# Attention over chunks, then routed tokens: the first pairs of heads enter the planned order

## The chip, the cores and the metric

The kernel runs on one core of a Trainium2 chip. The metric is the device time in microseconds of one execution. The profile is of one execution and spans the first to the last instruction. The engines are TensorE (PE, with its weight loads as PEld), VectorE (DVE), ScalarE (ACT), GpSimd (POOL) and SyncE (SP). Each works its own list of instructions in order, and waits only for results of the others and for transfers.

## The reference

The inputs q, k and v have 4 batches, 8 heads, 768 rows and 64 columns; mem_k and mem_v have 8 memory rows for each head. Attention is done in chunks of 32 rows with 16 rows of context to the left and 8 to the right; the result is the x of a layer that routes 128 tokens of each batch through two matrices of 512x1024 and 1024x512.

```python
for c in range(nc):
    ...
    k_full = np.concatenate([mem_k, k_ctx], axis=2)
    v_full = np.concatenate([mem_v, v_ctx], axis=2)
    scores = scale * np.matmul(q_c, k_full.transpose(0, 1, 3, 2))
    ...
    a = a / (np.sum(a, axis=-1, keepdims=True) + 1e-09)
    out[:, :, c_start:c_end] = np.matmul(a, v_full)
...
scores = np.einsum('bsd,d->bs', x, w_gate)
for b in range(B):
    top_idx = np.argpartition(-scores[b], capacity)[:capacity]
    xe = x[b, top_idx]
    h = np.maximum(xe @ w1, 0.0)
    ye = h @ w2
    g = 1.0 / (1.0 + np.exp(-scores[b, top_idx]))
    out[b, top_idx] = x[b, top_idx] + g[:, None] * ye
```

## The kernel before

**Units of work.** Two heads of one batch make a pair; there are 16 pairs, 0 to 15, four to a batch. Two pairs make a load unit, 0 to 7: one transfer each for q, k and v, issued on GpSimd's queue, which turns fp32 into fp16 on the way. Unit 0 comes in halves, one for each pair. Four buffers hold the units of each tensor, so unit 4 of k can be fetched only when both pairs of unit 0 have used theirs.

**Steps of a pair n.** Each is a function s_... and its name stands in a written order with its arguments. Kt, Qt and Vt are 16 transposes each on TensorE (line 278), of k, q and v; Kt and Vt share one PSUM tile, p_t. Kc, Qc and Vc copy the results to SBUF (lines 299 or 297, 289, 319); Kc is on VectorE unless the name ends in @ACT, Qc and Vc on ScalarE. Km and Vm write the memory columns (line 303). S.n.half are the score products (line 356), E.n.half their exponentials, three activations on ScalarE (line 363). T2 turns v back (line 328), V2 copies that. VV.n.half is the product with v (line 382), X.n.half the division by the sum on VectorE: a reciprocal and a multiplication (lines 387 and 394). Pairs take turns in four slots of SBUF buffers (n modulo 4).

**Steps of a batch b.** ST.b stores x (lines 449 and 451, on SyncE). D.b.i are the gate's dot products (line 456), R0 and R1 with R0c and R1c lay the scores out as rows, C.b.i compares every score with every other (line 513), CT counts (line 529), M, P, SL and SE make the selection (lines 541 to 559), A and AI the row numbers (line 570), F gathers the rows from the output (line 576), XT and XC transpose them, F1, H, F2 and Y are the two matrices (lines 603 to 624), and SC adds the result into the output (line 627). GE and G are the gate. For the last batch the names differ: X15, S14, S15 (scores), RL, C3, CT3, P3, and G0 with GB in place of a gather.

**What sets the order.** ORDER (lines 19 to 49) is a list of step names; the loop at line 685 calls them one after another, and so each engine gets its instructions in this order. An ending @DVE, @ACT or @POOL moves a copy to that engine. LU.u.t issues the load of unit u of tensor t, LW.i one of eight loads of the weights (lines 246 and 249), wg the two loads of the gate vector on SyncE (lines 638 and 639), gc builds gate columns from it. fill-i-step puts i products with zeros ahead of a step on TensorE (line 155): work of no use but to keep its clock up.

**The start.** Pairs 0 and 1 are not in the list: lines 644 to 675 call their first steps by hand, with 25 fills among them, twelve of them ahead of Kt.0. The memory rows come in by two loads on GpSimd's queue, cast on the way (lines 139 and 141), between those of pair 0, and mem_rows (line 198) transposes each and lays it down in memkT and memvT.

Of the kernel before, what the change touches and what calls it, by code (L numbers as in the profile page):

```python
# [16 lines left out]


ORDER = """
S.1.1 Vm.3 fill-1-VV.0.0 VV.0.0 Vm.4@DVE E.1.1 S.1.0 X.0.0 LU.4.k Kt.2 E.1.0 fill-1-Qt.2 Qt.2 Kc.2 VV.0.1 Qc.2  # L20
Km.2@POOL Kt.3 X.0.1 wg LU.4.q S.2.0 T2.1 Kc.3 E.2.0 S.2.1 V2.1 Vt.2 E.2.1 Km.3 LU.4.v VV.1.1 Vm.5@DVE Qt.3 X.1.1 Vc.2
VV.1.0 Qc.3 LW.0 gc Vt.3 S.3.0 X.1.0 Vc.3 T2.2 S.3.1 V2.2 E.3.0 LW.1 Kt.4 Vm.6@DVE VV.2.0 Kc.4 E.3.1 T2.3 X.2.0 Vt.4
LU.5.k V2.3 VV.2.1 Vc.4 Vm.7 Km.4@DVE Qt.4 X.2.1 Kt.6 Qc.4 VV.3.0 LU.5.q Kc.6@ACT S.4.0 X.3.0 T2.4 E.4.0 Km.6 Kt.5
V2.4 VV.3.1 LU.5.v D.0.2 Kc.5@ACT Qt.5 D.0.1 fill-1-S.4.1 S.4.1 Qc.5 Km.5 D.0.0 Kt.7 LU.6.q E.4.1 X.3.1 fill-1-S.5.1
S.5.1 Qt.6 Kc.7 ST.0 E.5.1 VV.4.0 D.0.4 LW.4 S.5.0 Km.7 D.0.3 Vt.5 Qc.6 D.0.5 LU.6.v Vc.5 fill-1-R0.0 R0.0 Vm.8@DVE
X.4.0 S.6.1 GE.0 E.5.0 T2.5 G.0 Vt.6 Vm.9 V2.5 VV.4.1 Vc.6 LW.2 R0c.0@DVE S.6.0 Qt.7 X.4.1 E.6.1 Kt.8 LU.7.k R1.0 Kc.8
Qc.7 VV.5.0 R1c.0 Km.8 Vt.7 X.5.0 E.6.0 T2.6 C.0.1 S.7.1 Vc.7 VV.5.1 V2.6 S.7.0 LW.3 C.0.0 E.7.1 Qt.8 X.5.1 Vt.10 Qc.8
C.0.3 fill-1-VV.6.1 VV.6.1 C.0.2 Vc.10 fill-1-S.8.0 S.8.0 C.0.5 E.7.0 T2.7 Vm.10@DVE C.0.4 LU.7.q Kt.9 X.6.1 V2.7@ACT
CT.0 Vm.11 LU.7.v Kc.9@ACT fill-2-S.8.1 S.8.1 M.0 fill-1-VV.7.1 VV.7.1 E.8.1 Km.9@DVE LU.6.k Vt.8 X.7.1 Qt.9 Vc.8 P.0
D.1.4 VV.7.0 Qc.9 D.1.3 Vt.9 LW.5 SL.0 Vc.9 X.7.0 fill-1-T2.8 T2.8 SE.0.0 VV.6.0 SE.0.2 V2.8@ACT Vm.12 SE.0.5 SE.0.1  # L30
SE.0.3 Kt.10 SE.0.4 X.6.0 E.8.0 A.0 fill-1-Qt.10 Qt.10 AI.0 D.1.0 ST.1 F.0 VV.8.1 Qc.10 D.1.2 S.9.0 Kc.10@ACT S.9.1
X.8.1 LW.6 Qt.11 D.1.1 E.9.0 VV.8.0 Km.10@DVE D.1.5 R0.1 Qc.11 X.8.0 S.10.1 Kt.11 E.9.1 R0c.1@DVE T2.9 Kc.11 R1.1
E.10.1 Vm.13 V2.9 fill-1-S.10.0 S.10.0 Vt.11 R1c.1@DVE E.10.0 Km.11@DVE VV.9.0 C.1.5 S.11.0 C.1.3 Vc.11 T2.10 C.1.2
fill-1-S.11.1 S.11.1 Vm.14 V2.10@ACT X.9.0 Vt.12 XT.0 C.1.1 Vc.12 VV.9.1 C.1.0 T2.11 XC.0 X.9.1 LW.7 Kt.13 GE.1 E.11.0
G.1 Vm.15 VV.10.0 V2.11 F1.0.0 E.11.1 X.10.0 Qt.12 Kc.13 H.0.0 VV.11.0 Qc.12 C.1.4 Km.13 Kt.12 X.11.0 fill-1-CT.1 CT.1
Kc.12 D.2.0 Km.12 T2.12 D.2.1 fill-2-VV.11.1 VV.11.1 V2.12@ACT D.2.2 M.1 Vt.13 X.11.1 P.1 S.12.1 Vc.13 fill-1-S.12.0
S.12.0 SL.1 SE.1.0 SE.1.5 VV.10.1 SE.1.3 E.12.0 SE.1.1 SE.1.4 T2.13 SE.1.2 X.10.1 A.1 E.12.1 Kt.14 AI.1 ST.2 D.2.3
VV.12.0 F.1 V2.13@ACT D.2.5 F1.0.1 X.12.0 Kc.14@ACT Qt.13 D.2.4 VV.12.1 Qc.13 H.0.1@DVE Km.14 Kt.15 X.12.1 GE.2 R0.2
Kc.15 fill-1-S.13.0 S.13.0 G.2 R0c.2 S.13.1 E.13.0 Vt.14 Km.15@DVE R1.2 Qt.14 R1c.2@DVE Vc.14 VV.13.0 C.2.4 Qc.14
F2.0.0 C.2.1 C.2.0 E.13.1 T2.14 C.2.3 F2.0.1 V2.14@ACT C.2.5 C.2.2 S.14.1 Y.0 S.14.0 X.13.0 fill-1-GV.14 GV.14 E.14.0  # L40
SC.0 CT.2 D3.0 D3.1 E.14.1 GVc.14 fill-1-VV.13.1 VV.13.1 D3.2 M.2 Vt.15 X.13.1 P.2 fill-1-Qt.15 Qt.15 Vc.15 SL.2 D3.3
fill-1-VV.14.0 VV.14.0 SE.2.3 Qc.15 SE.2.0 SE.2.2 SE.2.1 D3.5 XT.1 X16a T2.15 SE.2.4 XC.1@DVE S.15.0 X.14.0 F1.1.1
E.15.0 V2.15 S.15.1 S14.0 GV.15 H.1.1 D3.4 fill-1-VV.14.1 VV.14.1 GVc.15 E.15.1 SE.2.5 VV.15.0 X.14.1 A.2 S15.0
VV.15.1 AI.2 X15.0 F1.1.0 F.2 S14.1 X16b.0 ST.3.0 S15.1 RL.0 H.1.0@DVE GE.3 fill-1-RL.1 RL.1 RLc.0 G.3 fill-1-F2.1.0
F2.1.0 C3.0.0 RLc.1 C3.1.0 C3.2.0 C3.0.1 F2.1.1 C3.2.1 C3.1.1 C3.3.2 fill-2-CT3.0 CT3.0 Y.1 C3.5.2 C3.4.2 SC.1
fill-1-XT.2 XT.2 X15.1 CT3.1 XC.2 ST.3.1 G0 X16b.1 M.3 F1.2.0 fill-3-P3 P3 H.2.0 F1.2.1 SL.3 SE.3.5 SE.3.4 SE.3.0
SE.3.1 GB.0 SE.3.3 H.2.1 SE.3.2 GB.4 GB.2 F2.2.0 GB.5 F2.2.1 GB.1 Y.2@DVE GB.3 XC.3 SC.2 A.3 F1.3.0 AI.3 F1.3.1 H.3.0
F2.3.0 H.3.1 F2.3.1 Y.3@DVE SC.3
""".split()
# [679 lines left out]
```

The softmax here doesn't subtract the row's maximum and nothing guards it: scores larger than these inputs give would overflow.

## Time and profile before

| | |
|---|---|
| time, median of 3 runs | 133.36 us (132.72 to 134.24) |
| span of the profiled execution | 132.6 us |
| busy: TensorE, VectorE, ScalarE, GpSimd | 110.8, 87.6, 85.8, 44.4 us |
| DMA: GpSimd's queue, SyncE's queue | 13.04 MB and 61.0% of the 16 engines; 6.56 MB and 16.6% |
| read from and written to HBM | 24.25 MB, 7.34 MB |
| mean granted TensorE clock | 0.936 |

The bytes of a queue in the profile are counted as they land: a load that casts reads twice what it writes. A line of the list of groups or of the timeline names the engine, the source line, the operation, output<-input with shapes, and in brackets how long the engine stood idle before it and what ended that. Busy times are averages over stages of different kinds: a load stage (to about 72 us), an attention stage (to about 104 us) and the last batch's chain of small steps (to the end).

### The profile page before, as it was taken

The page shows a single profiled execution, that of the slowest core. Times are in us where ns is not written, and L with a number is a line of the kernel's source. Part 1 is how long each engine was busy: PE and PEld are TensorE (multiplying, and loading weights), DVE is VectorE, ACT ScalarE, POOL GpSimd, SP SyncE. Part 2 cuts the span into 40 slices and gives each one's busy share as a digit, 9 for nine tenths or more (in the row PEclk, how much of TensorE's full clock was granted, in tenths as well). Part 3 has the DMA queues.
Part 4 walks back from the last instruction along what each step waited for, and adds up shares of the span by engine and source line. Part 5 has one row for each costly group of instructions (what it writes and reads, how often), then busy time and mean ns, then how long its engine had stood idle before and what let it go on. Part 6 is the DMA issues. An engine that isn't in the chain of part 4 may idle for free. (4 is left out here: it accounts for less than half of the span.)

```text
span 132.6 us, 4756 instructions
## 1 busy us (share of the span) xinstructions
PE 110.8 (84%) x2038; PEld 81.0 (61%) x2038; DVE 87.6 (66%) x295; ACT 85.8 (65%) x163; POOL 44.4 (33%) x73
## 2 busy tenths in 40 slices
PE   6998998999999109999899999999999975998300
...
DVE  3443678879998902279899999899969893311200
ACT  4037879989999406699999838889877523115000
...
PEclk9999999999999965899999999999869999599995
DMA  2899999999999999999998200990320475902350
GB/s 57 137 181 188 205 205 206 210 203 208 209 270 289 261 206 208 207 206 207 300 270 147 45 7 0 271 236 17 41 43 2 127 153 144 173 1 23 61 74 6
DMA packets 16085, 19.90 MB, mean 150 GB/s; under 512 B 1152, under 2 KB 11840, under 8 KB 16064
## 3 DMA queue, kind: packets, MB, share of 16 engines
q0 software_dynamic: 12416, 13.04, 61.0%
q1 hardware_dynamic: 3648, 6.56, 16.6%
...
HBM read 24.25 MB, written 7.34 MB: 238 GB/s over the span
## 5 line engine op out<-in xcount | busy, mean ns | idle before, releaser
L363 ACT ACTIVATE es<-pss_S,maskb 128x256 f16<-128x256 f32 x96 | 37.9, 495 | 3.2 <-PE pss_S L356 2.8
L382 PE MATMUL pxx_VV<-vc,es 128*96 128x65 f16 (+3 forms) x360 | 23.1, 207 | 1.6 <-DVE x L394 0.6
L382 PEld LDWEIGHTS <-es 128*32 128x32 f16 (+1 forms) x384 | 20.2, 113 | 6.4 <-DVE x L394 1.5
L319 ACT COPY vw<-p_t 128x960 f16<-128x960 f16 x16 | 15.5, 969 | 7.7 <-PE p_t L278 7.6
L289 ACT COPY qT<-pvv_Qt 128x768 f16<-128x768 f16 x16 | 13.1, 821 | 7.1 <-PE pvv_Qt L278 7.0
L394 DVE TENSOR_TENSOR x<-pxx_VV,rd 128x384 f32<-128x384 f32 x30 | 16.7, 557 | 1.0
L627 POOL DMA_INDIRECT out_dram<-y,idx x4 | 6.6, 1638 | 25.1 <-issue 7.2
L456 DVE SCALAR_TENSOR_TENSOR junk<-x,wgb 128x512 f32<-128x512 f32 (+1 forms) x24 | 14.5, 635 | 0.1
L513 DVE TENSOR_SCALAR gr<-brow,scr 128x768 f16<-128x768 f32 (+1 forms) x27 | 13.9, 570 | 0.1
L278 PE MATMUL p_t<-ident,v 96*64 96x96 f16 x256 | 8.8, 213 | 5.9 <-DMA v<-in_v_dram 5.9
L387 DVE RECIPROCAL rd<-pxx_VV 128x6 f32<-128x6 f32 x30 | 5.7, 190 | 10.5 <-PE pxx_VV L382 10.0
L278 PEld LDWEIGHTS <-v 96*64 96x64 f16 x256 | 6.6, 113 | 7.5 <-DMA v<-in_v_dram 6.5
L356 PE MATMUL pss_S<-qT,kw 64*128 64x96 f16 x256 | 10.6, 207 | 0.0
L328 PE MATMUL pvv_T<-ident,vw 128*128 128x128 f16 x128 | 10.5, 228 | 0.0
L155 PE MATMUL p_f<-zeros 128*128 128x512 f16 x25 | 9.1, 501 | 1.3 <-DVE zeros L149 1.3
L299 DVE COPY kw<-p_t 128x1024 f16<-128x1024 f16 x11 | 7.5, 685 | 3.2 <-PE p_t L278 3.2
L356 PEld LDWEIGHTS <-kw 64*128 64x128 f16 x256 | 6.4, 95 | 5.2 <-issue 3.6
L278 PE MATMUL pvv_Qt<-ident,q 96*64 96x96 f16 x256 | 8.8, 213 | 0.6 <-DMA q<-in_q_dram 0.6
L155 PEld LDWEIGHTS <-zeros 128*128 128x128 f16 x57 | 5.5, 110 | 6.0 <-issue 3.0
L603 PEld LDWEIGHTS <-w_sb 128*128 128x128 f16 x128 | 8.3, 106 | 1.4 <-issue 0.6
L328 PEld LDWEIGHTS <-vw 128*128 128x128 f16 x128 | 8.0, 102 | 1.6 <-ACT vw L319 0.2
L278 PE MATMUL p_t<-ident,k 96*64 96x96 f16 x256 | 8.7, 212 | 0.1
...
## 6 DMA issues: line engine op xcount, KB each, us to landing
...
```

Of the source, the lines that this page charges most:

```text
L155: nc.tensor.matmul(out=ap, lhsT=zeros[:, 0:128], rhs=zeros, start=True, stop=True)
L278: nc.tensor.transpose(out=dst[64 * h:64 * h + 64, j, :], in_=src[n][:, h, 64 * j:64 * j + 64], identity=ident16[0:96, 0:96])
L289: nc.scalar.copy(out=qT, in_=half_view(bank("Qt", n))[:, :, 0:96].rearrange("p j t -> p t j"))
L319: nc.scalar.copy(out=vws[n % SLOTS].rearrange("p g (j t) -> p g j t", t=16)[:, :, :, 0:15], in_=_sap(p_t, 0, [[12, NG], [100, 8], [1, 15]]))
L328: nc.tensor.transpose(out=p_v[:, g, :], in_=vws[n % SLOTS][:, g, :], identity=ident16)
L356: nc.tensor.matmul(out=p_s[:, h, 96 * gi:96 * gi + 96], lhsT=kw[o:o + 64, g, :], rhs=qf[o:o + 64, 96 * g:96 * g + 96], start=True, stop=True)
L363: nc.scalar.activation(out=es[:, :, :, 32 * c:32 * c + 32], in_=pv[:, :, :, 32 * c:32 * c + 32], func=AF.Exp, bias=maskb[:, c:c + 1], scal ...
L382: nc.tensor.matmul(out=p_x[r0:r1, i, h, :], lhsT=es[:, h, gi, q0:q1], rhs=vc[:, GROUPS[half][gi], h, 0:w], start=True, stop=True)
L394: nc.vector.tensor_tensor(out=xs[b].rearrange("p g (n h d) -> p n g h d", n=NP, d=D)[:, pr, 3 * half:3 * half + 3], in0=px_view(n, half)[: ...
L456: nc.vector.scalar_tensor_tensor(out=junk[:, 0:c1], in0=xs[b][:, bl, 0:c1], scalar=1.0, in1=wgb[:, 0:c1], op0=ALU.mult, op1=ALU.mult, accu ...
L513: nc.vector.tensor_scalar(out=once(b, "gr", [128, NB, S], F16)[:, bl, c0:c1], in0=m.brow[:, c0:c1], scalar1=m.scr[:, bl:bl + 1], scalar2=N ...
L603: nc.tensor.matmul(out=bank("F1", b, half)[:, 128 * fi:128 * fi + 128], lhsT=w1_sb[:, dch, f0:f0 + 128], rhs=get(b).xeT[:, dch, :], start= ...
```

## The change

The first steps of pairs 0 and 1 move from the hand-written start into ORDER, and the whole list is laid out anew, with other fills and some copies on other engines. What stays ahead of the list is six fills, the memory rows' transposes with three fills between, three Vm and two fills. The memory rows are loaded on SyncE as fp32 and cast to fp16 by two copies on ScalarE, which takes two loads off GpSimd's queue; the second mem_rows uses another PSUM tile than the first (pvv in place of pmm), so that it need not wait for it. In the list the loads now come unit by unit: 4, weights 0 and 1, 5, weights 2 and 3, 6, weights 4 and 5, 7, weights 6 and 7, where before unit 6 was split around unit 7. The aim is a start that is planned like the rest and loads that arrive in the order of their use. The same steps run as before.

```diff
 ORDER = """
-S.1.1 Vm.3 fill-1-VV.0.0 VV.0.0 Vm.4@DVE E.1.1 S.1.0 X.0.0 LU.4.k Kt.2 E.1.0 fill-1-Qt.2 Qt.2 Kc.2 VV.0.1 Qc.2
-Km.2@POOL Kt.3 X.0.1 wg LU.4.q S.2.0 T2.1 Kc.3 E.2.0 S.2.1 V2.1 Vt.2 E.2.1 Km.3 LU.4.v VV.1.1 Vm.5@DVE Qt.3 X.1.1 Vc.2
-VV.1.0 Qc.3 LW.0 gc Vt.3 S.3.0 X.1.0 Vc.3 T2.2 S.3.1 V2.2 E.3.0 LW.1 Kt.4 Vm.6@DVE VV.2.0 Kc.4 E.3.1 T2.3 X.2.0 Vt.4
-LU.5.k V2.3 VV.2.1 Vc.4 Vm.7 Km.4@DVE Qt.4 X.2.1 Kt.6 Qc.4 VV.3.0 LU.5.q Kc.6@ACT S.4.0 X.3.0 T2.4 E.4.0 Km.6 Kt.5
-V2.4 VV.3.1 LU.5.v D.0.2 Kc.5@ACT Qt.5 D.0.1 fill-1-S.4.1 S.4.1 Qc.5 Km.5 D.0.0 Kt.7 LU.6.q E.4.1 X.3.1 fill-1-S.5.1
-S.5.1 Qt.6 Kc.7 ST.0 E.5.1 VV.4.0 D.0.4 LW.4 S.5.0 Km.7 D.0.3 Vt.5 Qc.6 D.0.5 LU.6.v Vc.5 fill-1-R0.0 R0.0 Vm.8@DVE
-X.4.0 S.6.1 GE.0 E.5.0 T2.5 G.0 Vt.6 Vm.9 V2.5 VV.4.1 Vc.6 LW.2 R0c.0@DVE S.6.0 Qt.7 X.4.1 E.6.1 Kt.8 LU.7.k R1.0 Kc.8
-Qc.7 VV.5.0 R1c.0 Km.8 Vt.7 X.5.0 E.6.0 T2.6 C.0.1 S.7.1 Vc.7 VV.5.1 V2.6 S.7.0 LW.3 C.0.0 E.7.1 Qt.8 X.5.1 Vt.10 Qc.8
-C.0.3 fill-1-VV.6.1 VV.6.1 C.0.2 Vc.10 fill-1-S.8.0 S.8.0 C.0.5 E.7.0 T2.7 Vm.10@DVE C.0.4 LU.7.q Kt.9 X.6.1 V2.7@ACT
...
-E.15.0 V2.15 S.15.1 S14.0 GV.15 H.1.1 D3.4 fill-1-VV.14.1 VV.14.1 GVc.15 E.15.1 SE.2.5 VV.15.0 X.14.1 A.2 S15.0
-VV.15.1 AI.2 X15.0 F1.1.0 F.2 S14.1 X16b.0 ST.3.0 S15.1 RL.0 H.1.0@DVE GE.3 fill-1-RL.1 RL.1 RLc.0 G.3 fill-1-F2.1.0
-F2.1.0 C3.0.0 RLc.1 C3.1.0 C3.2.0 C3.0.1 F2.1.1 C3.2.1 C3.1.1 C3.3.2 fill-2-CT3.0 CT3.0 Y.1 C3.5.2 C3.4.2 SC.1
-fill-1-XT.2 XT.2 X15.1 CT3.1 XC.2 ST.3.1 G0 X16b.1 M.3 F1.2.0 fill-3-P3 P3 H.2.0 F1.2.1 SL.3 SE.3.5 SE.3.4 SE.3.0
-SE.3.1 GB.0 SE.3.3 H.2.1 SE.3.2 GB.4 GB.2 F2.2.0 GB.5 F2.2.1 GB.1 Y.2@DVE GB.3 XC.3 SC.2 A.3 F1.3.0 AI.3 F1.3.1 H.3.0
-F2.3.0 H.3.1 F2.3.1 Y.3@DVE SC.3
+Kt.0 Kc.0@ACT fill-2-Qt.0 Qt.0 Qc.0 Km.0 Vt.0 Vc.0 fill-2-S.0.0 S.0.0 fill-1-S.0.1 S.0.1 E.0.0 Kt.1 Qt.1 Kc.1 E.0.1
+Km.1 Vt.1 Qc.1 Vc.1 fill-4-S.1.1 S.1.1 S.1.0 E.1.1 T2.0 Kt.2 V2.0 E.1.0 Kc.2 fill-1-VV.0.0 VV.0.0 Vm.3@POOL Qt.2 X.0.0
+Km.2@POOL Kt.3 Qc.2 LU.4.k VV.0.1 Kc.3 Vm.4 Qt.3 Km.3 wg X.0.1 Vt.2 LU.4.q Qc.3 S.2.0 S.2.1 Vc.2 T2.1 LU.4.v E.2.1
+V2.1 Kt.4 Vm.5 Kc.4 fill-1-T2.2 T2.2 E.2.0 LW.0 Vt.3 V2.2 Vm.6 VV.1.0 Vc.3 gc Km.4 Qt.4 S.3.0 X.1.0 Qc.4 LW.1 Vt.5
+Vc.5 VV.2.1 S.4.1 X.2.1 E.3.0 T2.3 LU.5.k Vt.4 V2.3 E.4.1 VV.2.0 Vm.7@DVE S.4.0 X.2.0 Vc.4 fill-1-Qt.5 Qt.5 LU.5.q
+fill-1-VV.1.1 VV.1.1 E.4.0 Kt.5 X.1.1 Qc.5 S.3.1 LU.5.v Kc.5 VV.3.0 E.3.1 Km.5 Qt.6 X.3.0 Vt.7 Qc.6 LW.2 fill-1-S.5.0
+S.5.0 D.0.2 Vc.7 fill-1-VV.3.1 VV.3.1 D.0.0 D.0.1 E.5.0 T2.5 X.3.1 LW.3 Kt.8 V2.5@ACT fill-1-S.5.1 S.5.1 Vm.9 Kc.8
+ST.0 D.0.3 E.5.1 Kt.7 Km.8 D.0.5 Qt.7 LU.6.k VV.5.0 Kc.7@ACT D.0.4 R0.0 X.5.0 LU.6.q GE.0 Qc.7 Vt.6 G.0 VV.5.1 Vc.6
+R0c.0@DVE LU.6.v T2.4 X.5.1 R1.0 V2.4@ACT Vm.8@DVE Kt.6 R1c.0@DVE Km.7@DVE Kc.6@ACT C.0.5 LW.4 fill-2-VV.4.1 VV.4.1
+C.0.2 Km.6 C.0.3 T2.6 C.0.0 S.7.0 LW.5 V2.6@ACT S.6.1 X.4.1 Vt.9 Vm.10 E.6.1 C.0.4 Qt.8 C.0.1 VV.4.0 LU.7.k Vc.9
+fill-2-CT.0 CT.0 X.4.0 E.7.0 LU.7.q fill-1-VV.6.1 VV.6.1 M.0 Qc.8 LU.7.v S.6.0 X.6.1 P.0 fill-1-S.8.1 S.8.1 E.6.0 SL.0
+T2.7 SE.0.3 SE.0.0 Kt.10 SE.0.2 E.8.1 Vm.11@DVE V2.7 S.7.1 fill-1-VV.6.0 VV.6.0 SE.0.5 Kc.10@ACT SE.0.4 SE.0.1 Qt.9
+X.6.0 A.0 E.7.1 Kt.9 Km.10@DVE AI.0 VV.7.0 Kc.9 F.0 Qc.9 fill-1-S.8.0 S.8.0 X.7.0 Vt.8 E.8.0 Km.9 D.1.2 T2.9 LW.6
+VV.7.1 D.1.1 Vc.8 Vm.13 V2.9 S.9.0 S.9.1 E.9.0 X.7.1 Kt.12 LW.7 T2.8 Kc.12 ST.1 E.9.1 VV.9.0 Vm.12 D.1.5 Km.12 Vt.11
+V2.8 Vc.11 X.9.0 fill-1-Qt.12 Qt.12 D.1.3 VV.8.1 Qc.12 D.1.4 Vt.13 X.8.1 T2.11 Vc.13 R1.1 D.1.0 VV.9.1 V2.11@ACT
+R1c.1@DVE Vm.15@DVE Kt.11 X.9.1 GE.1 R0.1 Kc.11 Qt.10 R0c.1@DVE Vt.10 Qc.10 G.1 VV.8.0 Vc.10 C.1.5 S.10.1 Qt.11 C.1.0
+E.10.1 Kt.13 C.1.3 fill-2-S.10.0 S.10.0 Kc.13 Qc.11 C.1.1 Vt.12 Km.13 E.10.0 Km.11@DVE T2.10 X.8.0 S.11.0 Vc.12 Vm.14
+V2.10 fill-2-S.11.1 S.11.1 C.1.2 E.11.0 fill-1-VV.10.0 VV.10.0 C.1.4 Kt.15 X.10.0 E.11.1 T2.12 Kc.15 fill-1-VV.11.0
+VV.11.0 V2.12 S.12.0 Km.15@DVE Qt.13 X.11.0 E.12.0 fill-1-CT.1 CT.1 D.2.1 Qc.13 D.2.2 VV.11.1 M.1 D.2.0 fill-2-S.13.0
+S.13.0 X.11.1 S.13.1 E.13.0 P.1 Qt.15 SL.1 SE.1.1 VV.12.0 SE.1.5 SE.1.4 Qc.15 SE.1.3 XT.0 SE.1.0 X.12.0 Vt.14 XC.0
+T2.13 SE.1.2 Vc.14 A.1 V2.13 VV.10.1 E.13.1 AI.1 S.12.1 X.10.1 F.1 F1.0.1 E.12.1 D.2.4 ST.2 VV.13.1 D.2.5 H.0.1 T2.14
+X.13.1 R1.2 V2.14@ACT D.2.3 Kt.14 VV.12.1 R1c.2@DVE GE.2 Kc.14 R0.2 X.12.1 Km.14 Qt.14 G.2 R0c.2 fill-2-VV.13.0
+VV.13.0 Qc.14 D3.3 C.2.4 F1.0.0 D3.5 C.2.0 S.14.1 H.0.0 C.2.1 S.14.0 GV.14 E.14.0 C.2.5 F2.0.0 GVc.14 E.14.1 C.2.3
+F2.0.1 X.13.0 Vt.15 Y.0 C.2.2 VV.14.0 Vc.15 D3.0 SC.0 CT.2 D3.2 D3.1 X16a D3.4 fill-1-T2.15 T2.15 M.2 X.14.0
+fill-1-P.2 P.2 V2.15@ACT S.15.0 SL.2 S.15.1 S14.0 XT.1 SE.2.0 E.15.0 SE.2.3 VV.14.1 SE.2.2 XC.1@DVE GV.15 SE.2.1
+SE.2.4 F1.1.1 E.15.1 GVc.15 X.14.1 VV.15.0 H.1.1 SE.2.5 S14.1 S15.0 A.2 VV.15.1 AI.2 X15.0 F.2 RL.0 S15.1 X16b.0
+ST.3.0 F1.1.0 X15.1 RLc.0 ST.3.1 X16b.1 fill-1-RL.1 RL.1 H.1.0@DVE GE.3 C3.0.0 F2.1.0 RLc.1 C3.1.0 C3.2.0 C3.0.1
+F2.1.1 C3.1.1 C3.2.1 C3.4.2 fill-2-CT3.0 CT3.0 Y.1 C3.5.2 C3.3.2 XT.2 SC.1 XC.2@DVE CT3.1 G.3 F1.2.1 M.3 fill-1-P3 P3
+H.2.1 G0 SL.3 SE.3.4 F1.2.0 SE.3.1 SE.3.5 SE.3.3 SE.3.2 SE.3.0 GB.1 H.2.0 GB.0 A.3 GB.5 AI.3 F2.2.0 F2.2.1 GB.3
+Y.2@DVE GB.4 GB.2 XC.3 SC.2 F1.3.0 F1.3.1 H.3.0 F2.3.0 H.3.1 F2.3.1 Y.3@DVE SC.3
 """.split()
...
     load_unit(0)
+    mem32 = [cst.tile([B * H, n_mem * D], FP, tag=f"mem32{i}", name=f"mem32{i}") for i in range(2)]
+    for t, src in zip(mem32, (mem_k, mem_v)):
+        nc.sync.dma_start(out=t, in_=_dap(src, 0, [[n_mem * D, B * H], [1, n_mem * D]]))
     load_half(k, k16s, 0)
+    load_half(q, q16s, 0)
     prow = cst.tile([128, 1], I32, tag="prow")
     nc.gpsimd.iota(prow, pattern=[[0, 1]], base=0, channel_multiplier=1)
-    load_half(q, q16s, 0)
     ident16 = cst.tile([128, 128], F16, tag="ident16")
     nc.gpsimd.memset(ident16, 1.0)
     nc.gpsimd.affine_select(out=ident16, in_=ident16, pattern=[[1, 128]], compare_op=ALU.is_equal, fill=0.0,
                             base=0, channel_multiplier=-1)
     memk16 = cst.tile([B * H, n_mem * D], F16, tag="memk16")
     memv16 = cst.tile([B * H, n_mem * D], F16, tag="memv16")
-    nc.gpsimd.dma_start(out=memk16, in_=_dap(mem_k, 0, [[n_mem * D, B * H], [1, n_mem * D]]))
     load_half(v, v16s, 0)
-    nc.gpsimd.dma_start(out=memv16, in_=_dap(mem_v, 0, [[n_mem * D, B * H], [1, n_mem * D]]))
     for src, dst in ((k, k16s), (q, q16s), (v, v16s)):
         load_half(src, dst, 1)
     for u in range(1, 4):
...
     nc.vector.memset(zeros, 0.0)
     warm = cst.tile([128, 1], FP, tag="warm")
     nc.scalar.activation(out=warm, in_=zeros[:, 0:1], func=AF.Exp)
+    nc.scalar.copy(out=memk16, in_=mem32[0])
+    nc.scalar.copy(out=memv16, in_=mem32[1])
     def fill_into(ap, n=1):
         for _ in range(n):
...
     memkT = cst.tile([128, n_mem, NPR], F16, tag="memkT")
     memvT = cst.tile([128, n_mem, NPR], F16, tag="memvT")
-    def mem_rows(src, dst):
-        p_mk = pmm.tile([128, n_mem, B * H], F16, tag="pm", name="p_mk")
+    def mem_rows(src, dst, pool, tag):
+        p_mk = pool.tile([128, n_mem, B * H], F16, tag=tag, name="p_mk")
         for j in range(n_mem):
             for hh in range(2):
                 nc.tensor.transpose(out=p_mk[64 * hh:64 * hh + 64, j, :], in_=src[:, D * j:D * j + D],
...
     s_gc = gate_columns
-    fill(12)
-    s_Kt(0)
-    s_Kc(0)
-    fill(2)
-    s_Qt(0)
-    s_Qc(0)
-    mem_rows(memk16, memkT)
-    s_Km(0)
-    fill(2)
-    s_Vt(0)
-    s_Vc(0)
+    fill(6)
+    mem_rows(memk16, memkT, pmm, "pm")
     fill(3)
-    s_S(0, 0)
-    s_E(0, 0)
-    mem_rows(memv16, memvT)
+    mem_rows(memv16, memvT, pvv, "pv")
     for n in range(3):
         s_Vm(n)
-    s_Qt(1)
-    s_Qc(1)
-    fill(2)
-    s_Kt(1)
-    s_Kc(1)
-    s_Km(1)
-    s_S(0, 1)
-    s_E(0, 1)
-    fill(2)
-    s_T2(0)
-    s_V2(0)
-    s_Vt(1)
-    s_Vc(1)
     fill(2)
     late_constants()
```

14 lines of the change are left out of this document (removed).

## The prediction

> **What bounds the kernel now.** I read the page's slices first (tenths of busy time in 40 slices of 3.3 us), then the waits around the one hole they show, then windows and timeline there.
>
> ```profile
> PE   6998998999999109999899999999999975998300
> DVE  3443678879998902279899999899969893311200
> ACT  4037879989999406699999838889877523115000
> PEclk9999999999999965899999999999869999599995
> DMA  2899999999999999999998200990320475902350
> ```
>
> Slices 13 to 16, counted from 0 (43 to 56 us): TensorE, ScalarE and VectorE fall together, while DMA stays full from 7 to 72 us. Before the hole ScalarE is the full one (8 to 9), after it VectorE (8 to 9, to 96 us). The waits of 43 to 57 us (engine, line, releaser: total, times, longest):
>
> ```profile
> PE p_t L278 <- DMA v<-in_v_dram: 5.9, 1, 5.9
> ACT vw L319 <- PE p_t L278: 5.7, 1, 5.7
> DVE rd L387 <- PE pxx_VV L382: 5.5, 1, 5.5
> DVE mask L541 <- PE pmm_CT L529: 2.8, 1, 2.8
> ```
>
> One wait, the transposes of v for a late pair, and the others hang on it. The windows price it (span, busy time per engine, granted TensorE clock, DMA share, GB/s):
>
> ```profile
> 42.00:45.00 3.00, 1.57 (x44) 1.18 (x38) 2.97 (x7) 2.51 (x5) 0.55 (x1) 1.00 1.13 287
> 45.00:48.00 3.00, 0.00 (x0) 0.00 (x0) 1.34 (x4) 0.00 (x0) 0.00 (x0) 0.88 1.22 216
> 48.00:51.00 3.00, 1.53 (x22) 1.19 (x23) 0.00 (x0) 0.58 (x1) 0.67 (x1) 0.50 1.24 206
> 51.00:54.00 3.00, 3.00 (x37) 2.06 (x38) 0.75 (x2) 1.75 (x5) 0.00 (x0) 0.50 1.21 208
> 54.00:57.00 3.00, 3.00 (x76) 2.25 (x74) 0.72 (x3) 2.45 (x5) 2.50 (x4) 0.98 1.20 208
> ```
>
> VectorE is busy 5.78 of these 15 us, 9.2 idle: the wait, then work fed to it at half clock. Which load it was: by its place in the order (after Qt.8, before VV.6.1) the step is Vt.10, which needs unit 5 of v. That was issued at 30.55 and took 18.9 us, landing at 49.45; the transposes start at 49.47. Last the tail:
>
> ```profile
> 103.32 1.00 POOL L576 DMA_INDIRECT xe<-out_dram,idx  x1 [8.76 <-DVE gate L572]
> 105.96 3.65 DVE L513 TENSOR_SCALAR gr<-brow,scr 128x384 f16<-128x384 f32 x9
> 110.80 0.40 PE L582 MATMUL pmm_XT<-ident,xe 128*128 128x128 f16 x4 [2.11 <-DMA xe<-out_dram,idx]
> 114.60 0.21 PE L545 MATMUL pss_P<-incl,ltri 128*128 128x1 f16 x1
> 125.40 1.56 POOL L627 DMA_INDIRECT out_dram<-y,idx  x1 [3.84 <-DVE y L622]
> ```
>
> From the last attention product on (102 us) it is one chain of small steps, 30 us long, with a gather in it.
>
> **What the skill says.** "TensorE: Matmul & The Clock Gate", section "What's actually happening": the array runs at half clock by default and after about 3.4 us of idleness, and needs about that long of work to come back. The trace agrees: 5.9 us idle, then 0.50 from 48 to 54 us; and the first fills come 0.43 us apart, later ones 0.21. "DMA: Bandwidth & Descriptors", section "SWDGE vs HWDGE vs iDMA": only GpSimd's transfers can cast, so a SyncE load brings fp32 and another engine must cast; all loads here that cast are on GpSimd's queue, as it says. The same page, "Issuing engines are not separate DMA queues": all queues share 16 DMA engines, so a store delays loads. Here unit loads of 384 KB land 1.95 us apart (k of unit 1 at 14.4, v of unit 4 at 35.9, eleven gaps), but with the first 1.5 MB store (issued 33.4) k, q of unit 5 came at 43.9 and 47.5: 5 us lost over the store. A weight load takes 1.3 us.
>
> **The change, part by part.**
>
> *Start.* GpSimd loses two issues (0.56 and 0.52 us), so v of pair 0 is issued some 0.6 us and pair 1 some 1.1 us earlier; the load stream, full from 5 us, should run about 0.7 us earlier. SyncE loads the memory rows first: the first packets of its present first transfer (issued 0.82) move at 1.9 us and 256 KB land at 4.8; 64 KB should land between 3 and 4.8, I take 3.3 and 3.8. The two casts are 32x512 on ScalarE: nearest row, fp32 128x512, 0.585 us; bounds 0.3 to 0.62, and ScalarE is idle from 2.3 to 8.2, so they cost nothing. TensorE: six fills of 0.43 end at 3.9, memory transposes (0.42 warm, up to 0.8 cold), three fills, transposes, two fills: 7.0 to 7.4. So Kt.0 slips from 6.65 to about 7.3; if the rows land at 4.8 it is 8.5. Behind Kt.0 wait Kc.0 (now ScalarE, 1.03), Qc.0 (0.82), Vc.0 (0.97): 7.9 + 2.8 = 10.7, then E.0.0 and E.0.1 back to back to 13.1 and Qc.1, Vc.1 to 14.9. Before, the same copies end at 15.8 without Kc.0 among them. wgb and wgT come 0.9 us later on SyncE; first use at 22 us.
>
> *The attention stage.* I add durations along each engine's order: E 1.20 (three activations), Qc 0.82, Vc 0.97, an ACT copy 1.03; VectorE copy 0.69, X 0.75 (0.19 + 0.56), dot 0.63, compare 0.58. Before, to Vt.10 ScalarE has 15 E, 8 Qc, 8 Vc, 2 copies and 0.6 of small work, 35.0 us; TensorE ran dry at 43.57, so clock = ScalarE sum + 8.55, with no room between. VectorE's sum there is 29.8 (14 copies, 12 X, 12 memory columns of 0.34, 6 dots, 2 compares, 2.1 others). To X.14.1 (ends 102.34) it is 80.2: 50.4 us of VectorE work in 58.8 us, less the 9.1 idle in the hole by the timeline, 49.7: factor 0.986.
> After: clock = ScalarE sum + 7.8 (Vc.0 ends at 10.7 with 2.85 of work done). At 43.57 that is 35.8, where VectorE's sum is 26.9: 10 copies, 11 X, 9 memory columns, 6 dots, 4 compares, 2.5 others. Left for VectorE to X.14.1: 79.4 - 26.9 = 52.5, times 0.986 = 51.8. X.14.1 ends at 43.6 + 51.8 = 95.4 if no load is waited for: 6.9 earlier. ScalarE alone (82.5 + 7.8 = 90.3) would allow less, so VectorE sets it. Totals hardly move (VectorE 91.8 to 91.6, ScalarE 91.1 to 89.6 by these sums; copies sent to ScalarE go from eleven to ten). Fills fall from 57 to 53: nothing, TensorE doesn't bind.
>
> *The loads.* New order: 4k 4q 4v LW.0 LW.1 5k 5q 5v LW.2 LW.3 6k 6q 6v LW.4 LW.5 7k 7q 7v LW.6 LW.7. With 1.95 and 1.3 us, 0.7 earlier, and 5 us for ST.0 (issued near 35.6): 5k 42, 5q 45, 5v 48, 6k 52.8, 6q 54.8, 6v 56.7; with ST.1 (issued near 55) 7k 65.5, 7q 67.6, 7v 70.5. Needed, by the later of the two sums: Kt.10 48, Kt.12 54 to 55.9, Vt.11 57, Qt.12 57, Vt.13 58 to 58.9, Kt.15 68, Qt.15 72.7, Vt.14 73.5. So the hole goes: Vt.10 now comes late, Kt.10 has 5 us in hand. Unit 6 has only 1 to 3 us, and ST.1 begins then. I charge 1.0 us for it (bounds 0 to 4.5, the upper one with a cold array behind it). Buffers free in time: LU.6 needs Kt.5, Vt.5, Qt.5, far ahead; the moved GpSimd copies (0.47) lie beside.
>
> *The tail.* VectorE's chain to the compares: before, X.14.1's start 101.55 to compares' start 105.96 is 4.4 us; after, X15.1 (0.55) and S14 go ahead of them, G.3 (0.65) behind: 4.3. Equal. But XT.2 stands ahead of CT3.1 on TensorE as before, so the gather (7.4 us) ends the wait for the counts; AI.2 now comes 2.0 us after X.14.1's start, before 1.55, and ST.3.1's 0.75 MB follow ST.3.0 at once: gather ready 0.5 to 2 us later by this clock. Behind it F1.2.1 and one fill stand ahead of P3 instead of F1.2.0, G0 and three fills (3.2 us from CT3.1 to P3 before, about 2 after). Net: -0.7 to +1.0; after P3 the same products are in another order. I charge 0.5.
>
> Sum: -6.9 (hole, cold array and start, with VectorE's larger remainder) + 1.0 + 0.5 = -5.4; 133.36 - 5.4 = 128.0.
>
> **Rivals.**
> 1. *Engines pack better* (0.20): no load wait, and VectorE, no longer fed at half clock, keeps its sum's pace times 0.93: 43.6 + 48.8 = 92.4, 10 us earlier; with 0.5 for the tail and some loss to loads, 125.0. For: VectorE's busy time is 0.92 of my sum. Against: after 57 us it already idled only 7%.
> 2. *The wait comes back at unit 6* (0.12): 3 us at Kt.12 or Vt.13 and a cold array (4.4 us at half clock cost about 1.7 before), less the 1.0 charged: +3.7 to 131.7, up to 132.5. For: DMA is full to 72 us in any order, and two weight loads now go ahead of unit 6. Against: the table above.
> 3. *Slower* (0.10): the memory rows come late, the array stays cold past 10 us (start +2), unit 6 waits (+4), and XT.2 holds the counts 3 us: 128.0 + 8 = 136.
> 4. The forecast (0.58): 128.0.
>
> **How the numbers follow.** Predicted is the likeliest, 128.0. The range 123.8 to 132.6 takes in 1 and 2 and the bounds of the unknown costs (casts nothing, load landing 0 to +4.5, tail -0.7 to +2), and leaves 3 out. Faster by over 1% (below 132.0): 0.58 + 0.20 + a third of 2, 0.81. Within 1%: the rest of 2, 0.09. Slower: 0.10.
>
> **What would show it.** No TensorE wait on a load above 2 us after 20 us; clock 1.00 from 10 to 90 us; Kt.0 near 7.3; E.1.1 starting near 15 instead of 15.7; X.14.1 ending near 96; 6k to 6v landing 53 to 58 and used at once; XT.2 again waiting for its gather, longer than 2.1. Wrong if TensorE waits on k or v of unit 6 for several us, if VectorE is idle over 10% from 45 to 95 us, or if the array is cold at the first pairs.

## The result and the profile after

The changed kernel took 126.3 us (median of four, 125.49 to 131.16) beside 133.8 us for the kernel before: ratio 0.945, 95% interval 0.934 to 0.956. A later measurement of both gave 0.935 (0.928 to 0.943). The forecast was 128.0, with a range of 123.8 to 132.6; rival 1 had 125.0. Single executions of one kernel differ by up to 9% with the granted clock, so a ratio here compares only executions within 1.5% of the fastest of their kernel, while a time is the median of all.

In the execution profiled beside that first measurement TensorE's array stood at half clock from 26 to 40 us, and its mean clock was 0.917. Thirteen of the other fourteen executions of this kernel had 0.946 or more, so the profile below is that of one of these (span 123.8 us, mean clock 0.975). Its slices, from the page (40 of 3.1 us each):

```profile
PE   5948879979999969996999999999999896879100
DVE  1830366865899975897999999899999897520200
ACT  6238977979999779997779965994799650313000
PEclk9999999999999999999999999999999999999955
DMA  2899999999999999999999950059406198604260
```

The hole is gone: from 9 us to the tail no slice has TensorE below 6, and from 5 us on the clock is full until TensorE has nothing left to do. DMA is full to about 71 us as before. The windows over the place of the old hole (columns as in the prediction):

```profile
42.00:45.00 3.00, 1.81 (x39) 1.39 (x37) 2.96 (x8) 1.72 (x2) 1.24 (x2) 1.00 1.14 294
45.00:48.00 3.00, 3.00 (x87) 2.55 (x85) 1.55 (x4) 2.91 (x7) 0.50 (x1) 1.00 1.12 276
48.00:51.00 3.00, 3.00 (x64) 2.23 (x63) 2.48 (x11) 2.87 (x8) 1.37 (x3) 1.00 1.16 212
51.00:54.00 3.00, 3.00 (x70) 2.33 (x71) 2.52 (x12) 3.00 (x6) 1.34 (x2) 1.00 1.23 205
54.00:57.00 3.00, 2.14 (x60) 1.83 (x56) 2.93 (x8) 2.12 (x5) 2.12 (x3) 1.00 1.25 208
```

VectorE is busy 12.44 of these 15 us, before 5.78. From 16 us to the tail TensorE's longest wait for a load is 0.53 us. The tail, in the timeline:

```profile
97.42 1.01 POOL L580 DMA_INDIRECT xe<-out_dram,idx  x1 [4.63 <-DVE gate L576]
99.54 3.64 DVE L517 TENSOR_SCALAR gr<-brow,scr 128x384 f16<-128x384 f32 x9
103.45 0.40 PE L586 MATMUL pmm_XT<-ident,xe 128*128 128x128 f16 x4 [0.98 <-DMA xe<-out_dram,idx]
105.47 0.17 PE L549 MATMUL pss_P<-incl,ltri 128*128 128x1 f16 x1
116.85 1.55 POOL L631 DMA_INDIRECT out_dram<-y,idx  x1 [4.13 <-DVE y L626]
```

XT.2 waits 0.98 us for its gather (2.11 before), and P3 comes 8.05 us after the gather's issue (11.28 before).

To compare the two orders at all points I took the start of VectorE's n-th division (the reciprocal that goes ahead of each X step; the 30th is X.14.1's), then the issue of the last scatter. Where two orders reach the same count isn't exactly the same work, but it is close from the 13th on. The 24th and the 30th, before and then after:

```profile
81.30 0.19 DVE L387 RECIPROCAL rd<-pxx_VV 128x6 f32<-128x6 f32 x1
101.55 0.20 DVE L387 RECIPROCAL rd<-pxx_VV 128x6 f32<-128x6 f32 x1
```

```profile
78.04 0.19 DVE L391 RECIPROCAL rd<-pxx_VV 128x6 f32<-128x6 f32 x1
95.32 0.19 DVE L391 RECIPROCAL rd<-pxx_VV 128x6 f32<-128x6 f32 x1
```

The stretches between:

| stretch | before, us | after, us | gain |
|---|---|---|---|
| to the 4th division | 23.1 | 27.1 | -4.0 |
| 4th to 13th (the hole) | 28.7 | 21.7 | +7.0 |
| 13th to 24th | 29.5 | 29.2 | +0.3 |
| 24th to 30th | 20.2 | 17.3 | +2.9 |
| 30th to the last scatter's issue | 23.9 | 21.55 | +2.35 |

The sum is 8.55 us, the distance between the two issues (125.40 and 116.85). The third line from the bottom is the odd one: the stretch from the 13th to the 24th isn't faster, although VectorE does more in it (27.35 us busy, before 24.80). Of the first line 1.3 us is a later first division, the rest is the new order, which puts more transposes and copies ahead of the third product (25.5 us, before 21.5).

How much of this comes with the clock? In the profile before, the array stood at half clock for 13.6 us between 7 us and the last scatter's issue, 6.8 of them directly behind the hole; in the one shown for none; in the first profile of the changed kernel for 17.1. The windows over this stretch, before and then in that first profile:

```profile
7.00:125.40 118.40, 105.17 (x2020) 79.02 (x2013) 85.01 (x273) 84.34 (x161) 37.20 (x59) 0.94 0.83 160
```

```profile
7.00:122.25 115.25, 104.26 (x1991) 79.96 (x1991) 84.36 (x268) 83.04 (x159) 36.08 (x59) 0.93 0.85 166
```

At about the same mean clock the new order is 3.15 us earlier at this point (one execution of each); with its own clock full, as in the profile shown, it is 8.55 us earlier. So a good part of the gain in the traces shown comes with the clock. The experiments ask what each line of the table is made of.

### The profile page after: what moved, and what is told of

Same layout as the page of the kernel before. It is cut to its first block, busy times and chain, and to the rows that moved or that the text cites. A ratio compares the mean times of both kernels' runs of the same rounds, so it can differ in the third digit from the quotient of the medians.

```text
span 129.4 us, 4740 instructions
## 1 busy us (share of the span) xinstructions
PE 109.7 (85%) x2034; PEld 81.9 (63%) x2034; DVE 88.0 (68%) x294; ACT 85.7 (66%) x163; POOL 43.3 (33%) x74
## 3 DMA queue, kind: packets, MB, share of 16 engines
q1 hardware_dynamic: 3744, 6.69, 16.5%
## 5 line engine op out<-in xcount | busy, mean ns | idle before, releaser
L386 PEld LDWEIGHTS <-es 128*32 128x32 f16 (+1 forms) x384 | 21.1, 116 | 5.5 <-DVE x L398 1.1
L517 DVE TENSOR_SCALAR gr<-brow,scr 128x768 f16<-128x768 f32 (+1 forms) x27 | 14.4, 589 | 0.0
L631 POOL DMA_INDIRECT out_dram<-y,idx x4 | 6.5, 1627 | 23.1 <-DVE y L626 10.4
L307 POOL COPY kw<-memkT 128x64 f16<-128x64 f16 x9 | 5.7, 630 | 18.8 <-DVE kw L303 15.9
L303 DVE COPY kw<-p_t 128x1024 f16<-128x1024 f16 x12 | 8.3, 688 | 3.4 <-PE p_t L282 2.6
L580 POOL DMA_INDIRECT xe<-out_dram,idx x3 | 3.1, 1032 | 21.1 <-DVE gate L576 10.6
L303 DVE COPY vc<-pvv_T 128x1024 f16<-128x1024 f16 x10 | 6.9, 688 | 4.3 <-PE pvv_T L332 4.3
L282 PEld LDWEIGHTS <-v 96*64 96x64 f16 x256 | 7.4, 117 | 3.5 <-issue 1.6
L282 PEld LDWEIGHTS <-k 96*64 96x64 f16 x256 | 7.0, 113 | 3.6 <-DMA k<-in_k_dram 2.1
```

Source lines behind the costliest of these rows:

```text
L282: nc.tensor.transpose(out=dst[64 * h:64 * h + 64, j, :], in_=src[n][:, h, 64 * j:64 * j + 64], identity=ident16[0:96, 0:96])
L303: {"DVE": nc.vector, "POOL": nc.gpsimd}[eng].tensor_copy(out=out, in_=in_)
L386: nc.tensor.matmul(out=p_x[r0:r1, i, h, :], lhsT=es[:, h, gi, q0:q1], rhs=vc[:, GROUPS[half][gi], h, 0:w], start=True, stop=True)
L517: nc.vector.tensor_scalar(out=once(b, "gr", [128, NB, S], F16)[:, bl, c0:c1], in0=m.brow[:, c0:c1], scalar1=m.scr[:, bl:bl + 1], scalar2=N ...
```

## The experiments

**The changed kernel again.** It was run unchanged, for a second trace.

> The changed kernel once more, for a trace with an undisturbed clock and as the comparison for the runs beside it. Theory A (the wait of Vt.10 for unit 5 of v was the loss, and the new order has no such wait): 125.5 to 126.5 us; no TensorE wait on a load above 1 us after 20 us; granted clock 1.00 from 10 to 90 us; X.14.1 ends near 96 us. Theory B (the start and a better packing of ScalarE and VectorE made the gain, the wait only moved): the same time, but load waits of 2 us or more at unit 6.

126.04 us (125.56 to 126.94); its trace is the one above.

**The hole alone, by moving the step.** In the kernel before, Vt.10 and Vc.10 go behind VV.6.0:

```diff
-... X.5.1 Vt.10 Qc.8 C.0.3 fill-1-VV.6.1 VV.6.1 C.0.2 Vc.10 fill-1-S.8.0 ...
+... X.5.1 Qc.8 C.0.3 fill-1-VV.6.1 VV.6.1 C.0.2 fill-1-S.8.0 ...
-... SE.0.0 VV.6.0 SE.0.2 V2.8@ACT Vm.12 ...
+... SE.0.0 VV.6.0 SE.0.2 Vt.10 V2.8@ACT Vc.10 Vm.12 ...
```

> The kernel before with one pair of steps moved: Vt.10 and Vc.10 go from behind Qt.8 to behind VV.6.0, loads untouched. Unit 5 of v still lands at 49.5 us, and Vt.10 is now due near 52 us. Theory A: the hole goes and with it the half clock behind it, 6 to 8 us less than before, 125.5 to 127.5 us, though the loads keep their order. Theory B: the wait comes back at a later load or the engines are no better packed, 130 us or more.

135.25 us (134.55 to 137.37), the kernel before 133.5 beside it (129.22 to 138.3): no gain. The hole did go: the 13th division came at 46.7 us instead of 51.8, the 18th at 60.0 instead of 65.6. Then TensorE met XT.0, the first product on gathered tokens (its timeline, and two of its windows):

```profile
71.80 0.61 PE L582 MATMUL pmm_XT<-ident,xe 128*128 128x128 f16 x4 [4.62 <-DMA xe<-out_dram,idx]
```

```profile
69.00:72.00 3.00, 0.20 (x3) 0.20 (x4) 0.00 (x0) 0.00 (x0) 0.00 (x0) 0.77 1.16 192
72.00:75.00 3.00, 3.00 (x41) 2.53 (x39) 1.52 (x6) 2.55 (x8) 0.46 (x1) 0.50 0.21 37
```

The gather was issued 5.8 us earlier than before (56.36, before 62.11) and still landed no earlier, at 71.75 us (70.69): it stands behind the loads on GpSimd's queue, the last of which landed at 71.1. In the kernel before, XT.0 came at 70.79, a tenth of a microsecond after its gather. So a second hole took the first one's place, with the array at half clock behind it, and the 20th division was at 73.3 (before 71.9). My theory that the hole by itself was worth its 5 to 7 us fell here.

**The hole alone, by moving the loads.** LW.0 and LW.1 go behind LU.5.v, so that unit 5 comes earlier:

```diff
-VV.1.0 Qc.3 LW.0 gc Vt.3 ... E.3.0 LW.1 Kt.4 ...
+VV.1.0 Qc.3 gc Vt.3 ... E.3.0 Kt.4 ...
-V2.4 VV.3.1 LU.5.v D.0.2 ...
+V2.4 VV.3.1 LU.5.v LW.0 LW.1 D.0.2 ...
```

> The kernel before with two weight loads (LW.0, LW.1) moved behind the load of unit 5 of v, all compute steps untouched. Two loads of 1.3 us less stand ahead of it. Theory A: it lands 2.6 us earlier (46.9 us), the wait falls from 5.9 to about 3.3 us, the time by 2.6 to 3.5 us to 130 to 131 us. Theory B: the time falls by under 1 us, as the engines behind it, not the wait, set the pace.

134.55 us (130.14 to 136.41): no gain either. v of unit 5 came 2.9 us earlier and more than halved the wait:

```profile
46.57 0.85 PE L278 MATMUL p_t<-ident,v 96*64 96x96 f16 x16 [2.48 <-DMA v<-in_v_dram]
```

The array stood at half clock from 47 to 60 us (47 to 54 before), XT.0 then waited 1.70 us, and the 20th division was at 73.1.

**The gather's step alone.** XT.0, XC.0, F1.0.0 and H.0.0 go later (XT.0 and XC.0 into SE.1, F1.0.0 and H.0.0 behind F.1), the hole stays.

```diff
-... Vt.12 XT.0 C.1.1 ... T2.11 XC.0 X.9.1 ... V2.11 F1.0.0 E.11.1 ... Kc.13 H.0.0 VV.11.0 ...
+... Vt.12 C.1.1 ... T2.11 X.9.1 ... V2.11 E.11.1 ... Kc.13 VV.11.0 ...
-... SE.1.0 SE.1.5 VV.10.1 SE.1.3 ... F.1 V2.13@ACT D.2.5 ...
+... SE.1.0 SE.1.5 XT.0 VV.10.1 XC.0 SE.1.3 ... F.1 F1.0.0 V2.13@ACT H.0.0 D.2.5 ...
```

> The kernel before with only XT.0, XC.0, F1.0.0 and H.0.0 moved later, Vt.10 as it was. Theory A2: the hole at 43 to 49 us stays and the gather was not waited for behind it: within 1 us of the kernel before. Rival: XT.0 held something even with the hole there, 2 us or more faster.

133.73, 134.09, 142.26 and 145.55 us beside 135.97 (132.75 to 140.16); ratio 1.007 (0.996 to 1.017): no difference. With the hole in front, the gather had just landed anyway.

**Both moves together.** The diff is the sum of the first and the third.

> The kernel before with two things moved: Vt.10 and Vc.10 as in the run that moved only them, and the first batch's gathered rows taken up later too (XT.0 and XC.0 from ahead of C.1.1 to ahead of VV.10.1, F1.0.0 and H.0.0 behind F.1). Theory A2: two DMA waits stand one behind the other, unit 5 of v for Vt.10 and the gather for XT.0, which lands near 71 us whatever TensorE does; taking away one runs into the other, taking away both gives the 5 to 7 us: 127 to 129 us, no TensorE wait on a transfer above 1.5 us between 40 and 90 us. Theory B (the packing of the new plan made the gain): 132 us or more, with other waits in their place.

135.38 us (132.1 to 138.05) beside 135.97 (132.75 to 140.16), where 127 to 129 was expected: no gain in the median. The execution that was profiled took 132.1, the shortest of the four, and its trace says where: the 24th division came level with the changed kernel (78.0; before 81.3).

```profile
78.14 0.20 DVE L387 RECIPROCAL rd<-pxx_VV 128x6 f32<-128x6 f32 x1
```

So in this trace the two waits together make up the 3.3 us that the table shows to that point. After it the lead went: the 30th was at 98.6 (95.3). VectorE waited 1.3 us for an F1 product, as F1.0.0 and F1.0.1 now follow each other, and XT.2 waited 2.54 us for its gather. One cost stands before the 24th as well: in all three traces with Vt.10 late (this one, the first and the next) the array is at half clock for 6.8 us from 56 to 58 us on, busy all the while and after no wait above 1.05 us. From the 17th to the 20th division this run took 10.7 us and the next 10.3, the kernel before 8.4.

**Both, with F1.0.0 and H.0.0 where the changed kernel has them.**

```diff
 (as both together, but F1.0.0 and H.0.0 leave the place behind F.1)
-... R1c.2@DVE Vc.14 VV.13.0 C.2.4 Qc.14 F2.0.0 C.2.1 C.2.0 E.13.1 T2.14 C.2.3 ...
+... R1c.2@DVE F1.0.0 Vc.14 VV.13.0 C.2.4 H.0.0 Qc.14 C.2.1 C.2.0 E.13.1 T2.14 F2.0.0 C.2.3 ...
```

> The kernel before with Vt.10, Vc.10, XT.0 and XC.0 late as in the run of both, and F1.0.0 with H.0.0 ahead of VV.13.0 instead of behind F.1, where the run of both lost 1.7 us of VectorE's time behind two F1 in a row on one PSUM bank. That run was level with the changed kernel up to the 24th division (78.1 us against 78.0) and fell behind after it. Theory: with this moved it stays within 1.5 us of the changed kernel to the 30th division (95.3 us there), 128 to 130 us in all. Rival: something else in the second half of the old order holds it, 131 us or more.

134.8 us (131.9 to 137.27), ratio 0.986 (0.975 to 0.998): a gain of 1.4%, at most 2.5, where 128 to 130 us was expected. In its trace the array stands at half clock from 56 to 63 and from 70 to 83 us while TensorE is busy, so the way to the 24th division (81.7) can't be compared. The rest can, as the clock is full from 83 to 110: from the 24th to the 30th it took 20.6 us, the run of both 20.5. The wait for the F1 product is gone, and one of 0.92 us for another product of TensorE (pvv_GV) has come; so that wait alone was not what held the run of both. Patches of the old order, three of them, don't make the new order.

**The load order.** In the changed kernel, LU.6.k goes behind LU.7.v:

```diff
-... Qt.7 LU.6.k VV.5.0 ...
+... Qt.7 VV.5.0 ...
-... Qc.8 LU.7.v S.6.0 ...
+... Qc.8 LU.7.v LU.6.k S.6.0 ...
```

> The changed kernel with one load out of order: k of unit 6 behind v of unit 7, as the kernel before had it. It would land near 66 us in place of 54; Kt.12, due near 54 to 57 us, waits for it. Theory A2 (what counts is that no step stands ahead of its transfer): a hole of 8 to 11 us with a cold array behind it, 8 to 12 us slower than the changed kernel, slower than the kernel before. Rival: the gain has little to do with the order of the loads, under 3 us slower.

142.62 us, ratio to the kernel before 1.059 (1.049 to 1.070); some 15 us slower than the changed kernel, where 8 to 12 was expected. k of unit 6 landed at 69.9 us instead of 54. The waits of 54 to 74 us:

```profile
DVE kw L303 <- PE p_t L282: 14.9, 1, 14.9
ACT vw L323 <- PE p_t L282: 14.6, 1, 14.6
PE p_t L282 <- DMA k<-in_k_dram: 13.3, 1, 13.3
```

One load seven transfers late takes three engines down together, and nothing makes it up: this is the old hole again, larger, with the array at half clock from 57 to 88 us. It shows what rival 2 would have looked like.

**The memory rows alone.** The kernel before, with only the SyncE loads and the ScalarE casts:

```diff
+    for t, src in zip(mem32, (mem_k, mem_v)):
+        nc.sync.dma_start(out=t, in_=_dap(src, 0, [[n_mem * D, B * H], [1, n_mem * D]]))
-    nc.gpsimd.dma_start(out=memk16, ...)
-    nc.gpsimd.dma_start(out=memv16, ...)
+    nc.scalar.copy(out=memk16, in_=mem32[0])
+    nc.scalar.copy(out=memv16, in_=mem32[1])
```

> The kernel before with only the memory rows' way changed (SyncE, fp32, cast on ScalarE); order and fills as before. Theory A2: GpSimd's two issues less don't move the loads, which are bound by the DMA engines; k of pair 0 lands 1 us later because the gate loads now fall among its packets; unit 5 of v still lands near 49.5 us and sets the hole's end: within 0.7 us of the kernel before. Rival (the forecast's): the load stream runs 0.7 us earlier, the hole ends 0.7 us earlier and the time falls by as much.

133.62 us (133.22 to 135.74), ratio 1.004 (0.996 to 1.012): no difference. The casts ran at 2.71 and 3.23 us, 0.62 each, and hid. But k of pair 0 came later, at 7.78 us by its first transposes (before 6.65):

```profile
7.78 0.80 PE L281 MATMUL p_t<-ident,k 96*64 96x96 f16 x16 [2.19 <-DMA k<-in_k_dram]
```

In this execution the array then stood at half clock from 7.9 to 14.7 us. The first division was at 19.8 (before 16.5), and the hole shrank by about as much (2.19 us of wait for v instead of 5.9, at 49.35), for v still came when it had. Here a late start cost nothing ahead of a load that sets the time.

**The gate's loads held back.** In the changed kernel two small memsets on VectorE keep wgb and wgT from the first microseconds, and gc goes later:

```diff
+        nc.vector.memset(wgb[:, 0:1], 0.0)
+        nc.vector.memset(wgT, 0.0)
-... Vc.3 gc Km.4 ...
+... Vc.3 Km.4 ...
-ST.0 D.0.3 E.5.1 ...
+ST.0 D.0.3 gc E.5.1 ...
```

> The changed kernel with the two gate vector loads on SyncE held back by two small memsets on VectorE at their place in the list (near 18 us in place of 1.7 us), and the gate columns built later. In the changed kernel k of pair 0 lands at 7.8 us, before at 6.65. Theory A: the gate loads' 256 KB and small packets are what delays it; it lands at 6.7 us, all of the start moves 1 us earlier, the time falls by 0.5 to 1.0 us. Rival: the first load is late for another reason (no change of its landing), or the start is hidden behind VectorE's backlog later on (landing earlier, time within 0.3 us).

125.87 us (124.79 to 132.81), the changed kernel 126.04 beside it: not told apart, though a gain of some tenths isn't ruled out. k of pair 0 landed at 4.9 us instead of 7.6; it was transposed at 6.15 instead of 7.63, no earlier because TensorE was at the fills and the memory rows until then, and the first division came at 16.2 instead of 17.8. So the gate's 257 KB, issued at 1.71 and 2.17 us, do hold up the first load, by 2.7 us, and TensorE by 1.5; the kernel was not shown to be faster without it.

**The same, with nine more single fills between X.0.0 and VV.2.0,** to keep the array from running short at the start:

```diff
-... Vm.3@POOL Qt.2 X.0.0 ... LU.4.k VV.0.1 ... T2.1 ... VV.1.0 ...
+... Vm.3@POOL fill-1-Qt.2 Qt.2 X.0.0 ... LU.4.k fill-1-VV.0.1 VV.0.1 ... fill-1-T2.1 T2.1 ... fill-1-VV.1.0 VV.1.0 ...
```

> The changed kernel with the gate loads held back as before and nine single fills more between X.0.0 and VV.2.0, where TensorE waits for loads in short pieces and where two of four profiles of this order show it at half clock for 14 us. Theory: the fills keep the array at full clock there and cost nothing, since TensorE waits anyhow; 0.5 to 1.0 us faster than the changed kernel in the median, and its slow profiles (129 us and more) go. Rival: the fills push the copies behind them back by 0.2 us each, 0.5 to 2 us slower.

and the changed kernel once more beside it:

> The changed kernel again, as the measure for the runs beside it: 125.5 to 126.5 us.

With the fills 127.86 us (127.3 to 130.81, six executions), ratio to the kernel before 0.951 (0.944 to 0.957); the changed kernel beside it 127.34 (125.29 to 133.71, six), above the 125.5 to 126.5 that was expected, with a ratio of 0.935 (0.928 to 0.943). In the medians the two hardly differ, and two of six executions with fills still took 129 us or more (two of six without); by the ratios the fills are slower. In the two traces the loss is not where I looked. The fills do push the work back: the first division is at 16.0 (the changed kernel 17.1), the 12th at 47.1 (45.9). Yet from the 17th (59.6 in both) to the 32nd (97.56 and 97.55, X15 counted in) the two agree within 0.1 us. What brings them together is a GpSimd copy that stands behind DMA issues. In the changed kernel's timeline and then in this one's:

```profile
56.62 0.52 PE L360 MATMUL pss_S<-qT,kw 64*128 64x96 f16 x16 [1.48 <-POOL kw L307]
```

```profile
56.60 0.51 PE L360 MATMUL pss_S<-qT,kw 64*128 64x96 f16 x16 [0.47 <-POOL kw L307]
```

The copy stands behind the gather's issue. GpSimd's instruction just ahead of that issue waits until k of unit 6 has landed, and the issue begins 0.84 us after the landing in both traces (landed 53.67 and 53.97 us, issued 54.51 and 54.80). So a load, through GpSimd's order, sets the time at 56.6 us, and being early or late by a microsecond before it only changes the wait, 1.48 or 0.47 us. It fits this that holding the gate's loads back gained so little. The loss in this trace is all in the tail, which begins with this wait:

```profile
104.83 0.44 PE L586 MATMUL pmm_XT<-ident,xe 128*128 128x128 f16 x4 [2.39 <-DMA xe<-out_dram,idx]
```

The gather, issued at 97.39 (97.40 in the changed kernel), took 7.4 us to XT.2 instead of 6.3; the clock fell to 0.68 between 104 and 107 us, and the last scatter came at 119.10 instead of 117.12. Why the gather took longer I can't say: the stores around it were issued at the same times within 0.1 us, and the second of them landed later as well (104.61, in the changed kernel 103.43).

**The tail's order.** In the changed kernel CT3.1 and P3 go ahead of XT.2, and XC.2 goes to ScalarE:

```diff
-... Y.1 C3.5.2 C3.3.2 XT.2 SC.1 XC.2@DVE CT3.1 G.3 F1.2.1 M.3 fill-1-P3 P3 H.2.1 G0 SL.3 SE.3.4 F1.2.0 ...
+... Y.1 C3.5.2 C3.3.2 CT3.1 G.3 M.3 fill-1-P3 P3 SL.3 XT.2 SC.1 XC.2 G0 SE.3.4 SE.3.1 SE.3.5 F1.2.1 H.2.1 F1.2.0 ...
```

> The changed kernel with XT.2 taken behind CT3.1 and P3 on TensorE (XC.2 on ScalarE), so that the last batch's counts no longer stand behind the gather of batch 2. Theory: CT3.1 starts at the end of the compares, about 0.7 us earlier than now in an undisturbed run, P3 about 2 us earlier; the time falls by 0.5 to 2 us against the changed kernel. Rival: F1.2 needs the gather itself and SC.3 waits for SC.2, so the end moves by less than 0.4 us.

129.78 us in the median: three executions at 129.49 to 130.27, one at 126.12 (the changed kernel 125.3 to 126.9 in most), so no gain in any. The profile, of one at 129.49, has P3 at 104.08 us, 1.4 earlier as meant, but four waits of 0.22 to 0.78 us follow in a row between 103 and 108, and then this window:

```profile
107.00:110.00 3.00, 2.53 (x25) 2.53 (x25) 0.00 (x0) 1.01 (x2) 0.00 (x0) 0.50 0.43 76
```

What was won on the counts was lost on products at half clock, from 105.5 to 112.4 us, though no single wait ahead of it was above 0.78. Of fifteen executions of the changed kernel three took over 129 us, here three of four; whether the edit brings the half clock about stays open, as one execution had none of the loss. It is only shown that the edit wins nothing.

## Why the prediction was right, and where its steps were wrong

The measured 126.3 us lies between the forecast's 128.0 and rival 1's 125.0, somewhat nearer the rival.

**The hole and X.14.1: right.** The step said that Vt.10 comes late enough, that VectorE's remaining work then sets the time, and that X.14.1 ends at 95.4. It ended at 96.1 us. From 50 to 95 us VectorE was busy 42.4 of 45 us, idle 6%; the clock was full from 5 to 117, though not in the first profile. From 43.57 us to the end of X.14.1 VectorE had 12.5 us of idle time before (46.3 of 58.8 us busy) and 4.7 after (47.8 of 52.5), so it was idle time that went, as the step said. The control is the load order: one load seven transfers late cost 15 us. What I hadn't seen is that the same 6 us can't be had from the hole alone: the two single cures of it gave nothing. In the old order XT.0 stood behind it, waiting for a gather that landed at 70.7 to 72.1 us however early TensorE was, and with the weights late the array stayed at half clock until 60 us besides. In the new order XT.0 comes at 77.9, 5 us after its gather has landed. The move of XT.0 was in the diff and I gave it no cost, so that the step holds for the new order is in part luck; in the old order, without that move the trace shows no gain up to the 24th division, with both moves 3.2 us.

**From the 24th to the 30th division: right in the sum, not reasoned.** The windows of this stretch, before, then with the memory rows alone (same order, no half clock), then after:

```profile
81.30:101.50 20.20, 19.88 (x372) 15.21 (x370) 17.90 (x66) 17.74 (x35) 3.79 (x3) 0.92 0.42 100
```

```profile
83.30:101.80 18.50, 18.30 (x372) 14.17 (x370) 17.63 (x66) 17.61 (x35) 3.52 (x3) 1.00 0.48 109
```

```profile
78.00:95.30 17.30, 16.95 (x332) 13.46 (x331) 16.43 (x64) 14.90 (x30) 3.27 (x3) 1.00 0.49 117
```

By them 1.7 of the 2.9 us is the half-clock stretch of the old profile (95 to 99 us), and 1.2 is VectorE work (17.63 against 16.43) that the new order has done earlier, in the middle, where VectorE is busy 27.35 us instead of 24.80. That is rival 1, engines that pack better, true in part. The first of the two is less sure: two further traces with these steps and 3.4 us of half clock in the stretch (Vt.10 late, and the weights late) took 19.9 us each, but only one with these steps has the full clock. That X.14.1 ended within 0.7 us of the forecast is owed in part to these 2.9 us, which the forecast had not reasoned.

**The tail: wrong.** The term was +0.5, because the gather would be ready 0.5 to 2 us later; measured was -2.35. As forecast more stores were issued behind the gather, 1.5 MB within 2.6 us, and it still took 6.0 us to XT.2 instead of 7.5, so the wait was shorter (0.98), not longer than 2.1. And the term left out the array: in all ten traces with a wait of 1.9 to 2.9 us at XT.2 it went to half clock (0.53 and 0.61 over 112 to 116 us before); in the three with 0.98, 1.10 and 1.26 it stayed at 1.00. The Trainium skill, "TensorE: Matmul & The Clock Gate", section "What's actually happening", gives some 3.4 us of idleness for that. Here half clock followed on a wait of 1.9 us at XT.2, with little work to either side, and in the run with the tail's order changed on shorter waits still. In every profile of the old order the gather took 7.3 to 7.7 us; in the new order it took 6.0 to 6.3 in three (a tail of 21.0 to 21.8 us from the 30th division) and 7.0, 7.4 and 7.9 in three, where the tail was about as long as before (23.35, 23.8 and 24.2 us; the last with k of unit 6 late). So the tail's gain isn't sure in each execution; what decides the gather's landing stays open.

**The load wait at unit 6: mis-sized.** The term was 1.0; TensorE waited for no load there. k, q and v of unit 6 landed at 53.8, 55.6 and 57.5 (in the first profile), within 1 us of the forecast, and in time. In its place stood what I had costed at nothing: Km copies on GpSimd behind DMA issues, 1.2 us of TensorE's time at 44.7 and 0.9 at 56.65. The first of them, with the issue that waited for a landing and the score product behind the copy:

```profile
43.40 0.79 POOL L253 DMA_DIRECT2D w_sb<-in_moe_w_dram  x1 [2.90 <-DMA k<-in_k_dram]
44.70 0.34 PE L360 MATMUL pss_S<-qT,kw 64*128 64x96 f16 x8 [1.19 <-POOL kw L307]
```

**The start: wrong, without effect.** The load stream was to run 0.7 us earlier; k of unit 1 landed at 15.5 in the first profile and at 16.3 in the one shown, instead of 14.4. Fewer issues on GpSimd's queue didn't help, because the gate's loads moved, on SyncE, in among k's first packets; with them held back k of pair 0 landed at 4.9 and k of unit 1 at 14.4. "DMA: Bandwidth & Descriptors", section "Issuing engines are not separate DMA queues", says that all queues interleave on the same engines; I had quoted it for stores and not applied it here. The memory rows landed at 2.7 and 3.2, earlier than the 3.3 and 3.8 I took, and the casts hid. Kt.0 came at 7.63 (forecast 7.3), E.1.1 at 15.2 (forecast near 15). All this came to a first division 1.3 us later, and none of it was seen to reach the end.

**The sum.** -6.9 was -6.2 by the table's first four lines, +1.0 was 0 (the copies that stood there in its place are within the -6.2), +0.5 was -2.35. Together 8.55 us in the traces and 7.5 in the medians, where 5.4 was forecast.

**Still open:** what of the new order's middle and tail the patched old order lacks. Its best, 0.986, leaves 4 to 5% unexplained by the three steps moved. The tail's 2.35 us is part of what it lacks, and the half clock from 56 to 58 us on is part of what it pays; why the array falls to half clock there in each of its traces is not known.
